# A decode kernel's ring of key and value slots: ten of 2 MB against five of 4 MB, with the output weights on a second queue

## The chip, the cores and the metric

The kernel runs on one core of one Trainium2 chip. Times are device microseconds of that core. A ratio is the mean time of one kernel's fast runs over that of the other's fast runs of the same rounds, so it is not quite the ratio of the medians that are quoted beside it. A 95% interval of a ratio is about 0.0015 either way here, or 4 us; single runs of one kernel mostly lie within 1 us of each other.

## The reference

One token (x, 512 numbers) goes through an attention block with 32 heads and a cache of 65,536 keys and values per head, and through a small gated feed-forward block; a gate mixes the two. Only the parts that matter:

```python
H, Sk, Dh = 32, 65536, 128                     # all arrays bf16
q = (x @ wq).reshape(1, 1, H, Dh)              # one query a head
scores = einsum("bhqd,bhkd->bhqk", q, k_cache) * Dh ** -0.5
o = einsum("bhqk,bhkd->bhqd", softmax(scores), v_cache)
a = o.reshape(1, 1, H * Dh) @ wo               # wo: 4096 x 512
b = (silu(x @ w_gate) * (x @ w_up)) @ w_down
out = g * a + (1 - g) * b                      # g = sigmoid((x * gate_w).sum())
```

K and V are 537 MB each and every byte is used once; all weights together are some 14 MB.

## The kernel before

It is written with hand-placed semaphores. SyncE issues all loads, in one fixed list, into a ring of ten slots of 2 MB (16 KB a partition). A row below is one contiguous run that a load moves into one partition; the trace has one record (a packet) for each row: 65,536 of 16 KB for the 512 loads of K and V, of 128 rows each. A slot holds 64 blocks of 128 keys. For a K slot, TensorE transposes 48 of the blocks and multiplies them with q, ScalarE copies the transposes out of PSUM, and VectorE scores the other 16 blocks by itself. V blocks follow some 15 groups behind. At the end come the projection with `wo`, one product a head, and the mix.

```python
NSLOT = 10; V_LAG = 2; ND = 16; SLOT = CB * 128           # CB = 64 blocks a slot
wo_dram = A_wo.rearrange("(h d) n -> d h n", d=Dh)        # rows of 512 numbers: 1 KB
def kv_src(t, i):                                         # 16 KB a partition, contiguous
    h, c = divmod(i, NCH)
    return t[0, h, c*CB*P:(c+1)*CB*P, :].rearrange("(p r) d -> p (r d)", p=P)

for s in range(NK - NCH - V_LAG, NK):                     # end of the job list
    if s == NK - NCH + min(2, NCH - 1):
        jobs += [("wo", i) for i in range(NOW)]           # NOW = 2
    jobs.append(("v", s))

# SyncE
for i, job in enumerate(jobs):
    if i >= NSLOT:
        for cond in free_of(jobs[i - NSLOT]):             # slot's last reader is done
            w(*cond)
    sp.dma_start(view(job), source(job)).then_inc(ld[i % NSLOT], 16)
# ... (cut)
# TensorE, end
while done_v < NV:
    if done_v == NV - VPC:                                # ahead of the last V slot
        w("s_otn", 1)
        for h in range(H - 1):
            out_proj(h)
    values(done_v)
    done_v += 1
```

## Time and profile before

| | before |
|---|---|
| time, median of 3 | 2,621.87 us (2,621.15 to 2,622.85) |
| bytes moved, mean rate over the span | 1,093 MB, 417 GB/s |
| TensorE, ScalarE, VectorE busy | 81%, 61%, 46% |
| last K or V byte, span of the trace | 2,609.0 us, 2,620.5 us |

First the page of the profile: the span, TensorE's busy time, the rate in 40 equal slices, packets, the share of each DMA queue (q1 is SyncE's queue, q8 fetches instructions), and the chain of work that ended last.

```profile
span 2620.5 us, 87632 instructions
...
PE 2120.4 (81%) x41281; PEld 2051.0 (78%) x41282; DVE 1208.0 (46%) x598; ACT 1585.7 (61%) x1607; POOL 25.3 (1%) x71
...
PE   6888878888888888888888888788787888888884
...
GB/s 397 425 424 425 425 426 425 425 425 425 426 424 426 424 426 425 425 426 425 425 422 422 421 421 419 421 420 424 419 419 420 418 424 419 421 420 418 421 370 276
DMA packets 81632, 1093.28 MB, mean 417 GB/s; under 512 B 8307, under 2 KB 14198, under 8 KB 15222
...
q1 hardware_dynamic: 81270, 1087.67, 98.6%
q8 instruction: 322, 5.28, 0.8%
...
DMA 82%; PE 15%; issue 1%; SPq 1%; ACT 1%; POOL 0%; DVE 0%; POOLq 0%; ACTq 0%
```

The loads bound it: the slices show a flat rate from beginning to end, and 82% of the chain is waiting for DMA. q8 deserves a look: 322 packets of 16 KB are 5.28 MB, and TensorE has 82,563 instructions (41,281 products and 41,282 weight loads), 256.4 for each packet.

Next the windows of the trace: busy time of each engine in a stretch, and at the end of the line the granted clock, the DMA share and GB/s.

```profile
400.00:1200.00 800.00, 658.25 (x12743) 642.54 (x12741) 372.60 (x179) 494.02 (x498) 6.25 (x20) 0.51 1.01 425
...
1600.00:2400.00 800.00, 656.58 (x12773) 641.19 (x12772) 374.35 (x180) 494.96 (x499) 6.41 (x20) 0.52 1.00 421
2541.00:2565.00 24.00, 15.35 (x400) 14.79 (x400) 5.57 (x4) 7.07 (x9) 0.64 (x2) 0.50 0.50 210
2577.00:2604.00 27.00, 7.47 (x256) 7.14 (x256) 0.00 (x0) 0.00 (x0) 0.00 (x0) 0.50 1.01 425
2609.00:2620.00 11.00, 8.95 (x91) 3.94 (x89) 0.90 (x2) 0.00 (x0) 0.00 (x0) 0.81 0.00 0
```

The rate is 425 GB/s early and 421 late. From 2,541 to 2,565 us it is 210, just half (the half-rate stretch). From 2,609 us on nothing is loaded.

What happens then is in the timeline of TensorE (start, duration, instruction):

```profile
2604.57 1.86 PE L442 MATMUL psT<-pcol,ring 128*128 128x1 bf16 x64 [2.89 <-DMA ring<-in_A_v_cache_dram]
2606.36 9.53 PE L470 MATMUL psT<-ring,oTn 128*1 128x512 bf16 x31
2615.82 1.75 PE L442 MATMUL psT<-pcol,ring 128*128 128x1 bf16 x64
2617.83 0.38 PE L496 MATMUL psT<-ring,oTn 128*1 128x512 bf16 x1 [0.26 <-DVE oTn L363]
```

The 31 projections (9.53 us) start only 2.6 us before the last V byte arrives, so the last V block waits behind them.

Last, the loads by line (KB each, median us from issue to landing). The last line is the output weights, on SyncE's queue like all others:

```profile
ring<-in_A_k_cache_dram SPq DMA_DIRECT2D x256, 2048.0 KB, 42.5
ring<-in_A_v_cache_dram SPq DMA_DIRECT2D x256, 2048.0 KB, 41.2
...
ring<-in_A_wo_dram SPq DMA_DIRECT2D x2, 2048.0 KB, 42.6
```

The single packet records of the trace, gathered by size, give the cost of a row of each length:

```
row         1,024 B   3,584 B   8,192 B   16,384 B   semaphore, 4 B   q8, 16,384 B
median ns        49       142       309        613                9          1,073
count         5,891     1,024       512     65,536            8,307            322
```

A 16 KB row begins 4 ns before the previous one ends, one in four takes 620 ns instead of 613, and the row that follows an instruction fetch takes 1,110 on average. No record names its DMA engine, but the rows in flight can be counted: sixteen in the stream (fifteen during a fetch), and in the half-rate stretch, where the DMA share is 0.50, eight, and seven during each of the three fetches that begin there (at 2,543.1, 2,551.2 and 2,557.6 us). So these fetches took the place of a row on one of the eight engines at work. The semaphore writes, 16 for each load, tell as much of the stream. From 200 to 1,200 us 125 fetches begin on q8; four trains of 204 writes each run through it with 4.89 to 4.91 us between writes, never set back, while others are set back 15 or 16 times (two followed 15 times, one 16), by 1.54 to 1.59 us, with one fetch begun each time. 125 fetches on eight engines are 15.6 each, on 16 they would be 7.8.

### The profile page before, as it was taken

What the parts mean: (1) busy time and instruction counts of PE and PEld (TensorE: products, weight loads), DVE (VectorE), ACT (ScalarE), POOL (GpSimd) and SP (SyncE); (2) the same over time, 40 slices, a digit from 0 to 9 for tenths busy, and PEclk for the clock granted to TensorE, in tenths of its full rate; (3) what the DMA queues carried; (4) which work ended last, traced back from release to release, by engine and by line L of the source; (5) the groups of instructions that cost most, each with busy time, mean ns of one, the idle gap of its engine ahead of it and who ended that gap; (6) DMA issues with size and microseconds to landing.
All of it is one profiled execution on the core that took longest, in us unless ns stands there. A gap on an engine that the chain in (4) does not pass through costs nothing.

```text
span 2620.5 us, 87632 instructions
## 1 busy us (share of the span) xinstructions
PE 2120.4 (81%) x41281; PEld 2051.0 (78%) x41282; DVE 1208.0 (46%) x598; ACT 1585.7 (61%) x1607; POOL 25.3 (1%) x71
## 2 busy tenths in 40 slices
PE   6888878888888888888888888788787888888884
PEld 4787777788778787878888878788787888787882
DVE  4744444444545454444444444444454444444440
ACT  4866666666666666666666666666666666666650
POOL 0000000000000000000000000000000000000000
PEclk8755565555555555555555555555555555555555
DMA  9999999999999999999999999999999999999986
GB/s 397 425 424 425 425 426 425 425 425 425 426 424 426 424 426 425 425 426 425 425 422 422 421 421 419 421 420 424 419 419 420 418 424 419 421 420 418 421 370 276
DMA packets 81632, 1093.28 MB, mean 417 GB/s; under 512 B 8307, under 2 KB 14198, under 8 KB 15222
## 3 DMA queue, kind: packets, MB, share of 16 engines
q1 hardware_dynamic: 81270, 1087.67, 98.6%
q8 instruction: 322, 5.28, 0.8%
q14 instruction: 40, 0.33, 0.0%
HBM read 1087.64 MB, written 0.00 MB: 415 GB/s over the span
## 4 chain that ended last, share of the span: by engine, by line
DMA 82%; PE 15%; issue 1%; SPq 1%; ACT 1%; POOL 0%; DVE 0%; POOLq 0%; ACTq 0%
DMA ring<-in_A_k_cache_dram 65%; DMA ring<-in_A_v_cache_dram 17%; PE psT L411 10%; PE psO L442 2%; PE psS L425 2%; SPq L220 1%; ACT KT L270 1%; PE psT L470 0%; PE psT L442 0%; PE psO L463 0%; PE psS L454 0%; POOL amx L235 0%; POOL nbias L237 0%; DVE finrow L366 0%; DVE mxs L338 0%
## 5 line engine op out<-in xcount | busy, mean ns | idle before, releaser
L270 ACT ACTIVATE KT<-psT 128x1024 bf16<-128x1024 bf16 x1536 | 1562.0, 1030 | 922.3 <-PE psT L411 921.7
L411 PE MATMUL psT<-ident,ring 128*128 128x128 bf16 x12288 | 1523.5, 303 | 412.1 <-DMA ring<-in_A_k_cache_dram 411.6
L411 PEld LDWEIGHTS psT<-ident,ring 128*128 128x128 bf16 x12288 | 1153.1, 137 | 432.8 <-DMA ring<-in_A_k_cache_dram 431.5
L329 DVE TENSOR_TENSOR prod<-ring,qbc 128x2048 f32<-128x2048 bf16 x256 | 586.7, 2292 | 1299.9 <-DMA ring<-in_A_k_cache_dram 1298.8
L442 PEld LDWEIGHTS psO<-pcol,ring 128*128 128x128 bf16 x15872 | 692.6, 111 | 54.0 <-DMA ring<-in_A_v_cache_dram 38.0
L442 PE MATMUL psO<-pcol,ring 128*128 128x1 bf16 x15872 | 690.2, 169 | 26.9 <-DMA ring<-in_A_v_cache_dram 25.4
L331 DVE TENSOR_REDUCE sD<-prod 128x16 f32<-128x2048 f32 x256 | 585.2, 2286 | 8.7
L425 PE MATMUL psS<-qTb,KT 128*128 128x1 bf16 x12288 | 540.9, 165 | 10.1 <-ACT KT L270 5.8
L425 PEld LDWEIGHTS psS<-qTb,KT 128*128 128x128 bf16 x12288 | 445.8, 104 | 18.2 <-ACT KT L270 17.7
L442 PE MATMUL psT<-pcol,ring 128*128 128x1 bf16 x512 | 14.8, 165 | 34.2 <-DMA ring<-in_A_v_cache_dram 34.2
L442 PEld LDWEIGHTS psT<-pcol,ring 128*128 128x128 bf16 x512 | 14.2, 103 | 35.2 <-DMA ring<-in_A_v_cache_dram 31.6
L251 ACT ACTIVATE pcol<-psS,nbias 128x512 bf16<-128x512 f32 x32 | 21.9, 684 | 30.2 <-POOL nbias L237 30.2
L235 POOL PARTITION_ALL_REDUCE amx<-mxs x32 | 14.1, 440 | 2236.9 <-DVE mxs L338 2236.9
L363 DVE TENSOR_TENSOR oTn<-psT,Li 128x1 bf16<-128x1 f32 x1 | 0.2, 161 | 49.8 <-PE psT L442 49.8
L338 DVE TENSOR_REDUCE mxs<-psS 128x1 f32<-128x512 f32 x32 | 22.1, 691 | 1.1
L258 ACT ACTIVATE qbc<-psT 128x512 bf16<-128x512 f32 x4 | 2.4, 597 | 21.2 <-PE psT L392 21.2
L237 POOL TENSOR_SCALAR nbias<-amx 128x1 f32<-128x1 f32 x32 | 10.0, 313 | 289.8 <-issue 289.8
L384 PE MATMUL psS<-xTb,ring 128*128 128x1 bf16 x128 | 3.6, 165 | 11.4 <-DMA ring<-in_A_wq_dram 11.4
L336 DVE COPY psS<-sD 128x128 f32<-128x128 f32 x32 | 9.1, 284 | 7.9 <-PE psS L425 7.9
L384 PEld LDWEIGHTS psS<-xTb,ring 128*128 128x128 bf16 x128 | 3.5, 104 | 11.5 <-issue 11.5
L470 PE MATMUL psT<-ring,oTn 128*1 128x512 bf16 x31 | 9.5, 481 | 0.0
L392 PE MATMUL psT<-ring,xb 128*128 128x512 bf16 x31 | 8.4, 438 | 0.2 <-issue 0.2
(39 smaller groups left out, 35.0 us busy)
## 6 DMA issues: line engine op xcount, KB each, us to landing
ring<-in_A_k_cache_dram SPq DMA_DIRECT2D x256, 2048.0 KB, 42.5
ring<-in_A_v_cache_dram SPq DMA_DIRECT2D x256, 2048.0 KB, 41.2
ring<-in_A_wq_dram SPq DMA_DIRECT2D x2, 2048.0 KB, 10.0
ring<-in_A_wo_dram SPq DMA_DIRECT2D x2, 2048.0 KB, 42.6
ring<-in_B_w_gate_dram SPq DMA_DIRECT2D x1, 1792.0 KB, 21.8
ring<-in_B_w_up_dram SPq DMA_DIRECT2D x1, 1792.0 KB, 25.7
ring<-in_B_w_down_dram SPq DMA_DIRECT2D x1, 1792.0 KB, 30.2
xrow<-in_A_x_dram SPq DMA_DIRECT2D x1, 1.0 KB
```

Source lines behind the costliest of these rows:

```text
L220: sp.dma_start(view(job), source(job)).then_inc(ld[i % NSLOT], 16)
L235: nc.gpsimd.partition_all_reduce(amx[:, h:h + 1], mxs[:, h:h + 1], P, RMAX).then_inc(sm["s_ar"], 1)
L237: nc.gpsimd.tensor_scalar_mul(nbias[:, h:h + 1], amx[:, h:h + 1], -SCALE).then_inc(sm["s_nb"], 1)
L251: nc.scalar.activation(pcol[:, h % 2, :], psS[:, h % 2, 0:NC_H], ACT.Exp, bias=nbias[:, h:h + 1], scale=SCALE, accum_out=rsum[:, h:h + 1]) ...
L270: nc.scalar.activation(KT[:, g % NKT, :], kt_ps(g), ACT.Copy, bias=0.0).then_inc(sm["ev_a"], 1)
L329: nc.vector.tensor_tensor(prod[:], kb, qb, ALU.mult).then_inc(sm["s_tt"], 1)
L331: nc.vector.reduce_sum(sD[:, h % 2, j * ND:(j + 1) * ND], prod[:], AX_X).then_inc(sm["s_rd"], 1)
L338: nc.vector.reduce_max(mxs[:, h:h + 1], psS[:, h % 2, 0:NC_H], AX_X).then_inc(sm["s_mx"], 1)
L411: last = nc.tensor.transpose(dst[:, k * 128:(k + 1) * 128], src[:, b * 128:(b + 1) * 128], ident[:])
L425: last = mm(psS[:, h % 2, col:col + 1], KT[:, g % NKT, k * 128:(k + 1) * 128], qTb[:, h:h + 1], start=True, stop=True)
L442: last = mm(acc, src[:, b * 128:(b + 1) * 128], pcol[:, h % 2, col:col + 1], start=(j == 0 and b == 0), stop=(j == NCH - 1 and b == CB - 1))
L470: mm(psT[0:1, 0, 0:D], oTn[:, h:h + 1], view(("wo", h // HO))[:, h % HO, :], start=(h == 0), stop=(h == H - 1))
```

## The change

Its intent is fewer and longer rows: five slots of 4 MB with 32 KB a partition. Along with it `wo` moves to ScalarE's queue, the projection moves ahead of the penultimate V slot, the last V slot comes in 3.5 + 0.5 MB, x and gate_w come transposed through ScalarE's queue, and the other weights are laid out in long rows. The core of the diff:

```diff
-NSLOT = 10
+CB_MAX = 128
+NSLOT = 5
+SHARE = 4
+DB = 16
-V_LAG = 2
+V_LAG = 1
+TAIL = 16
-    CB = min(64, NC_H)
+    CB = min(CB_MAX, NC_H)
+    ND = CB // SHARE                  # 32 of 128 blocks on VectorE, as two of 16
-        wd_dram = B_w_down.rearrange("(c p) n -> p c n", p=P)
+        wd_dram = B_w_down.rearrange("(p c) n -> p c n", p=P)   # also wq, w_gate, w_up
-        for s in range(NK - NCH - V_LAG, NK):
-            if s == NK - NCH + min(2, NCH - 1):
-                jobs += [("wo", i) for i in range(NOW)]
-            jobs.append(("v", s))
+        rest = [("v", s) for s in range(NK - NCH - V_LAG, NK)]
+        early = max(0, len(rest) - (NSLOT - NOW))
+        jobs += rest[:early] + [("wo", i) for i in range(NOW)] + rest[early:]
+            if job == ("v", NK - 1):
+                cut = (CB - TAIL) * 128
+                return [(dst[:, 0:cut], src[:, 0:cut]), (dst[:, cut:], src[:, cut:])]
 # SyncE
-            sp.dma_start(xrow[0:1, :], ...); sp.dma_start(gwrow[0:1, :], ...)
+            for job in jobs:
+                if job[0] != "wo":
+                    load(sp, w, job)
 # ScalarE
+            act.dma_start(xT[:, 0:Dc], ...); act.dma_start(gwT[:, 0:Dc], ...)
 ... (cut: softmax, copies out of PSUM)
+            for job in jobs:
+                if job[0] == "wo":
+                    load(act, w, job)
             softmax(H - 1)
 # TensorE
-                if done_v == NV - VPC:
-                    w("s_otn", 1)
-                    for h in range(H - 1):
-                        out_proj(h)
+                if done_v in proj_at:          # ahead of the penultimate slot
+                    out_proj(proj_at[done_v])
 ... (cut: slot views, gate by two small products, VectorE in halves)
```

## The prediction

> **What bounds it.** The loads. The chain of waits is 82% DMA; the page moves 1,093 MB at 417 GB/s, DMA share 1.0 in nearly every slice; TensorE is 81% busy, ScalarE 61%, VectorE 46%, and they wait for K (VectorE 1,299 us). A faster engine gives nothing.
>
> The packet records give more. A 16 KB row takes 613 ns and the next starts 4 ns before its end; an 8 KB row takes 309: almost no cost per packet is left. Every fourth descriptor is 7 ns longer, and the 4-byte semaphore write costs about 6 ns a transfer. By my reading the instruction fetches (322 of 16 KB, second queue) fall on half of the 16 DMA engines: each takes 1,066 ns and the load packet after it 1,110, about 1.5 us of its engine, some 60 us for each of eight. That half sets the pace. The other runs ahead: the windows show 425 GB/s to 1,200 us, then 421 when the lead has used up the ring, and 210 (eight engines) from 2,541 to 2,565 us, when the next V slots wait for the last head's softmax. Estimate for a lagging engine: 4,096 packets x 611.7 ns + 62 us of fetches + 35 us of weights = 2,603 us, near where the stream ends (2,608). So the half-rate stretch costs little.
>
> After the last byte 11.5 us remain: 31 projections begun at 2,606.4 take 9.5 us, then the last V block, the row and the store.
>
> **What the change does.**
> 1. 32 KB rows, half the descriptors: saves (estimate) 22 ns, perhaps 30 more, of 9,868 per 4 MB: 6 us, at most 15, all critical. If rows are split into 16 KB packets, nothing.
> 2. w_down in 14 KB instead of 1 KB rows: 1 us.
> 3. Projection ahead of the penultimate V slot and a 0.5 MB tail: after the last byte only 16 products, one projection (0.4), the row (0.7) and the store: 4 us instead of 11.5. Saves 7.
> 4. First transfer issued 0.7 us earlier.
> 5. Five slots of 4 MB hold the same bytes. K is held about 22 us, V 16 us, of 39 us before the slot is needed (estimate from TensorE's load): no slot comes late.
> 6. The last V loads no longer wait for the last softmax: as argued, worth little.
> 7. The risk: the output weights (4 MB in 1 KB rows, 256 packets an engine) come through ScalarE's queue beside V's 32 KB rows. [...] Here a load packet after another queue's packet takes 376 to 490 ns more. If turns are by single rows, the weights end after the last V: 33 turns x 0.4 us, plus the projection and two V slots behind it, some 35 us lost. If a turn takes many small rows, nothing. The same holds for x and gate_w in 8-byte pieces at the start (0 to 6 us). I hold the benign case likelier, 2 to 1.
>
> **Prediction.** Benign 2,601 us, bad 2,637. I say 2,603 us, range 2,588 to 2,635; over 2% faster 0.03, within 2% 0.94, over 2% slower 0.03.
>
> **What would show it.** K and V packets of 32 KB at about 1,220 ns; 422 to 424 GB/s late in the run; no half-rate stretch; the end 4 us after the last V byte; output weights landing before V's penultimate slot. Wrong if: 32 KB packets take under 1,215 ns (faster), the weights' landing takes over 50 us, ScalarE's last exponential waits behind its own issue, or fetches cost less between larger packets.

That two queues take turns, and how many rows a turn has, was the author's assumption: in the kernel before, all loads are on one queue, and no run had shown it. Nor had one shown whether a 32 KB row would stay one packet. The 376 to 490 ns are measured there: a 16 KB row takes 378 ns more (median) after an 8 KB fetch of q14, another instruction queue, and 489 more after one of q8.

## The result, and the profile after

| | before | after |
|---|---|---|
| time, median | 2,621.93 us | 2,612.85 us (2,612.24 to 2,613.41) |
| ratio | | 0.9965 (0.9948 to 0.9982) |
| span of the trace | 2,620.5 us | 2,610.4 us |
| last K or V byte | 2,609.0 us | 2,580.3 us |
| last byte of any load | 2,609.0 us | 2,590.3 us |
| from there to the end | 11.6 us | 20.0 us |

The time lies within the range, but the gain is 9 us where 19 were predicted. The page after:

```profile
span 2610.4 us, 87113 instructions
...
PE 2090.8 (80%) x41279; PEld 2035.5 (78%) x41280; DVE 1204.8 (46%) x597; ACT 1580.7 (61%) x1607; POOL 101.2 (4%) x71
...
GB/s 410 426 426 429 428 427 427 428 427 426 428 423 426 421 424 424 424 422 423 422 423 425 423 423 422 423 424 423 422 423 423 421 426 419 425 421 425 425 387 258
DMA packets 42344, 1093.23 MB, mean 419 GB/s; under 512 B 4481, under 2 KB 8578, under 8 KB 8706
...
q1 hardware_dynamic: 37586, 1083.46, 97.8%
q8 instruction: 322, 5.28, 0.8%
q10 hardware_dynamic: 4400, 4.20, 0.5%
...
DMA 68%; PE 28%; issue 1%; DVE 1%; another core or an unknown queue 1%; ACT 0%; POOL 0%; ACTq 0%; POOLq 0%
```

The rate is up a little in most slices (in ten of the 40 it is lower, by 1 to 4 GB/s and in the last by 18) and there are half as many packets (a row of 32 KB stayed one: the trace has 32,768 of them). A new queue, q10, stands for ScalarE's loads. The chain is less DMA (68%) and more TensorE (28%). It does not say that TensorE got slower, as its busy time fell by 30 us; that much of it is a matter of names, since TensorE now waits for V where it waited for K, is a reading that no run tested.

The windows:

```profile
400.00:800.00 400.00, 328.11 (x6413) 322.89 (x6411) 187.12 (x90) 248.36 (x251) 15.80 (x10) 0.50 1.00 427
1600.00:2400.00 800.00, 652.28 (x12831) 641.33 (x12829) 374.30 (x180) 495.82 (x502) 34.59 (x21) 0.51 1.00 423
2544.00:2574.00 30.00, 9.67 (x339) 9.36 (x339) 0.55 (x2) 0.78 (x2) 0.81 (x2) 0.50 1.00 415
2574.00:2591.00 17.00, 0.05 (x1) 0.09 (x2) 0.00 (x0) 0.00 (x0) 0.00 (x0) 0.50 0.83 283
2591.00:2611.00 20.00, 16.77 (x288) 9.77 (x287) 0.90 (x2) 0.00 (x0) 0.00 (x0) 0.67 0.01 2
```

423 GB/s late instead of 421. At the end a tail appears: from 2,574 to 2,591 us the loads run at 283 GB/s, and TensorE does nothing (0.05 us). Then it is busy 16.8 us of the last 20.

The chain of waits at the end (start, duration, what it was):

```profile
2566.02 24.79 another core or an unknown queue
...
2590.95 9.50 PE psT L509 x31
2600.45 6.75 PE psT L479 x256
...
2607.43 0.60 PE psT L533
```

"Another core or an unknown queue" is here the transfer on ScalarE's queue, the output weights. TensorE waits 24.79 us for them. Only then come the 31 projections, both V slots behind them (256 products), and the last projection. TensorE's timeline says it by name:

```profile
2590.95 9.50 PE L509 MATMUL psT<-ring,oTn 128*1 128x512 bf16 x31 [24.93 <-DMA ring<-in_A_wo_dram]
2600.38 6.80 PE L479 MATMUL psT<-pcol,ring 128*128 128x1 bf16 x256
2607.43 0.59 PE L533 MATMUL psT<-ring,oTn 128*1 128x512 bf16 x1 [0.25 <-DVE oTn L400]
```

Lines answering to those of the loads before (the third is the large part of the last V slot):

```profile
ring<-in_A_k_cache_dram SPq DMA_DIRECT2D x128, 4096.0 KB, 34.7
...
ring<-in_A_wo_dram ACTq DMA_DIRECT2D x1, 4096.0 KB, 50.2
ring<-in_A_v_cache_dram SPq DMA_DIRECT2D x1, 3584.0 KB, 32.2
```

A 4 MB load on SyncE's queue lands in some 30 us. The output weights, issued at 2,540.6 us, take 50.2.

The packet records show why. Of the 1 KB rows of the weights, 376 were read from 2,544 to 2,571 us, beside 337 of V's rows of 28 or 32 KB: nearly one for one. When the large part of the last V slot had landed at 2,578.6 us, 2,877 of the 4,096 rows of the weights were still to come; they took to 2,590.3. At the start it is the same: x comes in 128 rows of 8 bytes, as does gate_w, and from 4 to 22 us 221 of ScalarE's small rows were read beside 220 rows of 32 KB of the other queue. x landed 13.6 us after its issue and gate_w 23.9; in the kernel before both were there at 2.5 us.

So here the two queues took turns row by row (376 beside 337, 221 beside 220), which was the case that the prediction held to be the less likely. But V's rows of 32 KB that began from 2,544 to 2,571 us took only 1,253 ns on average (1,237 in the stream from 1,000 to 2,000 us, fetches included), not the 0.4 us more that the prediction had taken from rows after an instruction fetch.

### The profile page after: what moved, and what is told of

It reads as the page before. It is cut to its first block, busy times and chain, and to the rows that moved or that the text cites. A ratio compares the mean times of both kernels' runs of the same rounds, so it can differ in the third digit from the quotient of the medians.

```text
span 2610.4 us, 87113 instructions
## 1 busy us (share of the span) xinstructions
PE 2090.8 (80%) x41279; PEld 2035.5 (78%) x41280; DVE 1204.8 (46%) x597; ACT 1580.7 (61%) x1607; POOL 101.2 (4%) x71
## 4 chain that ended last, share of the span: by engine, by line
DMA 68%; PE 28%; issue 1%; DVE 1%; another core or an unknown queue 1%; ACT 0%; POOL 0%; ACTq 0%; POOLq 0%
DMA ring<-in_A_v_cache_dram 67%; PE psT L444 17%; PE psO L479 5%; PE psS L460 4%; DMA gwT<-in_gate_w_dram 1%; DVE prod L371 0%; DVE sD L374 0%; PE psT L479 0%; ACT KT L304 0%; PE psT L509 0%; PE psT L425 0%; PE psS L494 0%; PE psS L418 0%; PE psO L502 0%
## 5 line engine op out<-in xcount | busy, mean ns | idle before, releaser
L479 PEld LDWEIGHTS psO<-pcol,ring 128*128 128x128 bf16 x15872 | 703.1, 112 | 450.1 <-DMA ring<-in_A_v_cache_dram 349.6
L267 POOL PARTITION_ALL_REDUCE amx<-mxs x32 | 71.8, 2242 | 2085.2 <-DVE mxs L381 2085.2
L269 POOL TENSOR_SCALAR nbias<-amx 128x1 f32<-128x1 f32 x32 | 28.3, 883 | 357.2 <-issue 357.2
L479 PEld LDWEIGHTS psT<-pcol,ring 128*128 128x128 bf16 x512 | 13.8, 102 | 12.5 <-ACT pcol L285 9.4
## 6 DMA issues: line engine op xcount, KB each, us to landing
ring<-in_A_k_cache_dram SPq DMA_DIRECT2D x128, 4096.0 KB, 34.7
ring<-in_A_v_cache_dram SPq DMA_DIRECT2D x127, 4096.0 KB, 29.4
ring<-in_A_wo_dram ACTq DMA_DIRECT2D x1, 4096.0 KB, 50.2
```

The source lines that it names most:

```text
L267: nc.gpsimd.partition_all_reduce(amx[:, h:h + 1], mxs[:, h:h + 1], P, RMAX).then_inc(sm["s_ar"], 1)
L269: nc.gpsimd.tensor_scalar_mul(nbias[:, h:h + 1], amx[:, h:h + 1], -SCALE).then_inc(sm["s_nb"], 1)
L479: last = mm(acc, src[:, b * 128:(b + 1) * 128], pcol[:, h % 2, col:col + 1], start=(j == 0 and b == 0), stop=(j == NCH - 1 and b == CB - 1))
```

## The experiments

Twelve kernels were run, all timed over five rounds against the kernel before. Theory A: the row-by-row turns put the weights behind V, and TensorE's order makes two V slots wait for them. Theory C: TensorE's instruction fetches fall on eight of the 16 DMA engines, and those set the pace of the stream. Their rivals are named with each run.

| run | median us | ratio to before (95%) | last byte of a load | end after it |
|---|---|---|---|---|
| changed kernel | 2,612.85 | 0.9965 (0.9948 to 0.9982) | 2,590.3 | 20.0 |
| e1_wo_sp | 2,599.75 | 0.9916 (0.9903 to 0.9930) | 2,592.1 | 6.0 |
| e2_proj_last | 2,606.72 | 0.9943 (0.9929 to 0.9957) | 2,592.7 | 12.5 |
| e3_rows16_sp | 2,621.16 | 0.9999 (0.9987 to 1.0012) | 2,613.8 | 6.0 |
| e4_one_tail | 2,601.19 | 0.9922 (0.9908 to 0.9935) | 2,591.5 | 7.2 |
| e5_pe_more | 2,636.94 | 1.0056 (1.0039 to 1.0074) | 2,631.1 | 7.0 |
| e6_pv_thin | 2,577.85 | 0.9832 (0.9819 to 0.9844) | 2,572.1 | 3.9 |
| e7_share48 | 2,596.78 | 0.9902 (0.9890 to 0.9915) | 2,589.8 | 5.9 |
| e8_share64 | 2,618.30 | 0.9987 (0.9974 to 0.9999) | 2,606.9 | 6.0 |
| f1_x_sp | 2,613.37 | 0.9967 (0.9952 to 0.9981) | 2,592.0 | 20.3 |
| f2_share48_x_sp | 2,593.74 | 0.9894 (0.9881 to 0.9906) | 2,586.0 | 5.9 |
| f3_best | 2,593.37 | 0.9889 (0.9876 to 0.9901) | 2,586.7 | 4.8 |
| g1_pe_more48 | 2,601.78 | 0.9922 (0.9908 to 0.9936) | 2,594.4 | 6.0 |

The last two columns are from the profiled run of each.

### e1_wo_sp: the output weights back on SyncE's queue

```diff
 # SyncE
             for job in jobs:
-                if job[0] != "wo":
-                    load(sp, w, job)
+                load(sp, w, job)
 # ScalarE
-            for job in jobs:
-                if job[0] == "wo":
-                    load(act, w, job)
             softmax(H - 1)
```

> The changed kernel with one part undone: the output weights are issued by SyncE again, in their place of the job list. Theory A (row-by-row turns between two queues let the weights land 8 us after the last V byte, and TensorE, which projects ahead of the penultimate V slot, then has 9.5 us of projection and 6.8 us of V products behind them): the weights land before V, nothing but 16 products and one projection follows the last byte, and the time is 2,592 to 2,597 us. Rival B (the DMA engines that carry the instruction fetches are busy to the end anyway, so the place of the weights does not matter): 2,609 to 2,614 us, as the changed kernel.

It took 2,599.75 us, 13.1 less than the changed kernel. TensorE's timeline at the end:

```profile
2575.03 9.23 PE L505 MATMUL psT<-ring,oTn 128*1 128x512 bf16 x31
2584.19 3.41 PE L475 MATMUL psT<-pcol,ring 128*128 128x1 bf16 x128
2591.32 3.57 PE L475 MATMUL psT<-pcol,ring 128*128 128x1 bf16 x128 [3.72 <-DMA ring<-in_A_v_cache_dram]
2595.15 0.58 PE L529 MATMUL psT<-ring,oTn 128*1 128x512 bf16 x1 [0.25 <-DVE oTn L396]
```

The projections now start at 2,575.0, 16 us earlier, while V still comes in, and end before the last slot is there. That is what theory A said, and it is shown: this one edit is worth 13 us. The time missed the expected stretch by 3 us, in two places. The end is 6.0 us after the last byte and not 4 (see e4). And the last byte came no sooner than in the changed kernel (2,592.1 against 2,590.3 us), so the turns cost the DMA engines next to nothing: rival B was right on that half. What was lost was TensorE's work, put behind a transfer that came last.

Two windows of the same run show the half-rate stretch again, and the end:

```profile
2539.00:2545.00 6.00, 5.61 (x162) 5.52 (x159) 0.99 (x2) 3.04 (x3) 0.38 (x1) 0.50 0.52 171
2592.00:2598.00 6.00, 3.48 (x110) 2.89 (x107) 0.90 (x2) 0.00 (x0) 0.00 (x0) 0.50 0.01 3
```

From 2,539 to 2,545 us only 1 KB rows were read, about 165 in a microsecond, at a DMA share of 0.52. A row takes 46 to 48 ns, so (estimate) 165 x 0.047 = 7.8, some eight engines, were at it, and eight had nothing to do.

### e2_proj_last: the projection after all V products

```diff
             while done_v < NV:
-                if done_v in proj_at:
-                    out_proj(proj_at[done_v])
                 values(done_v)
                 done_v += 1
+            for i in range(NOW):
+                out_proj(i)
```

> The changed kernel (weights still from ScalarE) with the 31 projections after all V products instead of ahead of the penultimate slot. Theory A: the weights still land near 2,591 us, V's products are done by then, and only 9.5 us of projection and about 3 us of ending follow: 2,604 to 2,607 us, so projecting ahead costs some 7 us as long as the weights come late. If the order of TensorE's work does not matter: 2,612 to 2,614 us.

2,606.72 us, 6.1 less than the changed kernel, as theory A has it: the V products are done before the weights land, and the projections alone wait for them.

```profile
2581.59 3.57 PE L479 MATMUL psT<-pcol,ring 128*128 128x1 bf16 x128 [6.94 <-DMA ring<-in_A_v_cache_dram]
2593.33 9.39 PE L509 MATMUL psT<-ring,oTn 128*1 128x512 bf16 x31 [8.16 <-DMA ring<-in_A_wo_dram]
```

Projecting early is right when the weights are early (e1) and wrong when they are late: the changed kernel combined the early projection with the queue that makes the weights late.

### e3_rows16_sp: five slots of 4 MB, but rows of 16 KB

Each slot's load is cut into its two halves, on e1_wo_sp (the waits count 32 instead of 16):

```diff
-            return [(dst, src)]
+            half = CB * 64
+            return [(dst[:, 0:half], src[:, 0:half]), (dst[:, half:], src[:, half:])]
```

> As e1_wo_sp, but every 4 MB K or V slot comes in two transfers of 16 KB a partition row. Theory A (the gain in the stream is from half as many descriptors: 1,216 against 2 x 613 ns, one 7 ns stretch in every four descriptors, one semaphore write a transfer, together 70 ns per 4 MB or 18 us): 14 to 18 us slower than e1_wo_sp. Rival B (the gain is from the five larger slots or from the other weights' layout): within 3 us of e1_wo_sp.

2,621.16 us: 21.4 more than e1_wo_sp, a little over the expected 14 to 18, and as slow as the kernel before. The window of the late stream:

```profile
1600.00:2400.00 800.00, 641.69 (x12730) 631.59 (x12727) 370.37 (x179) 491.00 (x498) 30.68 (x20) 0.53 1.00 419
```

419 GB/s, where the changed kernel has 423. So the longer rows, in transfers twice as large, carry all of the stream's gain (the run halves both and does not separate them), and larger slots with the old rows are no better than the ten small ones, rather worse: the last byte comes at 2,613.8 us against 2,609.0. The records account for 18 us (estimate): rows overlap by 4 ns, so a 32 KB row costs 1,212 ns and two of 16 KB 1,218, which is 48 ns per 4 MB; the 7 ns stretches and the semaphore writes, half as many, make some 22 more; 70 ns times 256 slots. The rest of the 21.4 us is open; rows of 16 KB that met no fetch took 614.5 ns on average instead of 614.2, which is 1.4 us of it.

### e4_one_tail: the last V slot in one transfer

```diff
-            if job == ("v", NK - 1):
+            if False:                      # and no wait for the tail's semaphore
```

> As e1_wo_sp, but the last V slot comes in one transfer. If the ending counts, 128 products (3.6 us) instead of 16 (0.5 us) follow the last byte: 2.5 to 3.5 us slower than e1_wo_sp. If TensorE is late anyway: the same as e1_wo_sp.

2,601.19 us: 1.4 more than e1_wo_sp, half of what was expected. The timeline of e1_wo_sp above has the reason: at 2,591.32 TensorE makes all 128 products of the last slot in one go (3.57 us). Its wait ended with the large first part, which landed only 1.3 us before the 0.5 MB tail (2,590.84 and 2,592.11 us in the packet records), so 112 products, not 16, were left at the end. So the tail was worth about the time that it takes to load, here 1.3 us.

### e6_pv_thin: fewer TensorE instructions

On e1_wo_sp:

```diff
-                for k in range(GB):
+                for k in (0, GB - 1):      # two V products of eight
```

> As e1_wo_sp, wrong on purpose: of every eight V products only the first and the last are made, 24,576 fewer TensorE instructions and all loads as before. Theory C: 96 fewer fetches, 18 us faster than e1_wo_sp (9 us if spread over 16 engines), about 2 us of it the shorter last V block on top. Rival D, bytes: only those 2 us.

2,577.85 us, 21.9 less than e1_wo_sp, with the very same loads. (The comparison with the reference doesn't notice the thinned sum, and the kernel is not valid.) q8 and the late window:

```profile
q8 instruction: 226, 3.70, 0.6%
```

```profile
1600.00:2400.00 800.00, 473.54 (x9112) 459.07 (x9112) 374.51 (x181) 479.77 (x507) 29.32 (x20) 0.71 1.00 426
```

322 fetches became 226, and 423 GB/s became 426. The last byte came 20.0 us earlier (the rest is the shorter last V block): 0.21 us for each of the 96 fetches. Theory C expected 1.53 us / 8 = 0.19; spread over 16 engines it would have been 0.10. The rows of V and K themselves took 1,216 ns as before, so TensorE's fewer products made no row faster. Rival D falls. One rival was not named: with fewer products the slots also come free sooner. It is not likely: the K and V loads of e1_wo_sp landed 34.7 and 29.4 us after their issue (medians), and one slot takes 9.9 us at 423 GB/s, so as a rule (estimate) two loads were already queued in front, and a slot that is free sooner would not have helped the DMA engines that are behind.

### e5_pe_more and g1_pe_more48: more TensorE instructions

```diff
+                for _ in range(12):
+                    pe.wait_ge(sm["s_ident"], 1)     # satisfied long ago
                 for k in range(GB):                  # one group of transposes
```

> As e1_wo_sp, with 12 waits that are already satisfied ahead of every group of transposes: 9,216 more TensorE instructions and not a byte or a product more. Theory C (TensorE's instruction fetches, 16 KB for each 256 instructions, cost 1.04 us on their DMA engine and 0.49 us more for the load packet after them, and all fall on the same eight engines, which set the pace): 36 more fetches x 1.53 / 8 = 6.9 us slower than e1_wo_sp, or 3.4 us if they are spread over all 16. Rival D (the pace is set by bytes, or by the compute engines' use of the on-chip memory): within 1 us of e1_wo_sp.

2,636.94 us, 37 more, and with runs from 2,627 to 2,647. The 36 more fetches came (358 on q8), but TensorE itself was now late. Two lines of its waits:

```profile
PE psT L442 <- issue: 152.7, 282, 2.2
...
PE psO L477 <- issue: 104.1, 105, 2.7
```

Where e1_wo_sp waits 415 us in total for V, this run hardly waits for data and stands 328 us in "issue". It is inconclusive for theory C. It was repeated on f2_share48_x_sp (below), where TensorE has more room:

> f2_share48_x_sp with the 12 satisfied waits of e5_pe_more ahead of each of its 1,280 groups of transposes, some 7,700 more TensorE instructions: e5_pe_more repeated where TensorE has room (72% busy instead of 80%), since there TensorE itself became late. Theory C (instruction fetches on eight engines set the pace): 30 more fetches x 1.53 us / 8 = 5.7 us slower than f2_share48_x_sp, 2,598 to 2,601 us (2.9 us if all 16 engines share them). Rival D (bytes set the pace): 2,593 to 2,595 us. If it is 10 us or more slower, TensorE is late again and the run says nothing of the fetches.

2,601.78 us, 8.0 more than f2_share48_x_sp, with 30 more fetches (320 against 290):

```profile
q8 instruction: 320, 5.24, 0.8%
```

TensorE still waited 311 us for K and 128 us for V, so it was not late on the whole. The direction is theory C's; the time is just over the expected 2,598 to 2,601 us, and the size, 0.27 us a fetch, is above its 0.19. Some 75 us of new "issue" waits may hold the rest, which is not shown. Together with e6: fewer fetches, faster; more fetches, slower; no byte of data changed in either.

### e7_share48 and e8_share64: fewer TensorE instructions, right result

On e1_wo_sp, VectorE scores more blocks of each K slot:

```diff
-    ND = CB // SHARE
+    ND = 3 * CB // 8        # e7: 48 blocks     (e8: CB // 2, 64 blocks)
```

> As e1_wo_sp, right result: VectorE scores 48 of the 128 blocks of a K slot instead of 32, so TensorE makes 16 fewer transposes and 16 fewer score products a slot, 8,192 fewer instructions. Theory C: 32 fewer fetches, 6 us faster than e1_wo_sp, 2,593 to 2,595 us. Rival D: the same as e1_wo_sp. VectorE rises from 46% to about 69% busy and is not in the way.

> As e7_share48 with 64 of 128 blocks on VectorE: 16,384 fewer TensorE instructions than e1_wo_sp. Theory C: 64 fewer fetches, 12 us faster than e1_wo_sp, 2,587 to 2,589 us, if VectorE keeps up (estimate 18.6 us of work in each 19.8 us). If VectorE frees the K slots too late, slower than e7_share48.

e7 took 2,596.78 us, 3.0 less than e1_wo_sp where 6 were expected. Its window from 120 to 200 us:

```profile
120.00:200.00 80.00, 72.81 (x1464) 72.57 (x1465) 71.84 (x34) 54.76 (x57) 2.56 (x2) 0.50 0.94 397
```

397 GB/s there instead of 428: VectorE, busy 90% of this stretch, started at 38 us, after gate_w had come, and gave its first slots back late. e8 took 2,618.30 us: the same loss at the start is larger (332 GB/s from 120 to 200 us), and its last byte came 14.7 us later than e1's (VectorE is 94% busy from 2,500 to 2,540 us, and the loads fall to 340 GB/s in the 40 us after). The expectation "12 us faster" failed: VectorE kept up in the middle (426 GB/s from 400 to 2,400 us) but not at the two ends.

### f1_x_sp, f2_share48_x_sp and f3_best: x and gate_w first on SyncE's queue

```diff
 # ScalarE
-            act.dma_start(xT[:, 0:Dc], ...); act.dma_start(gwT[:, 0:Dc], ...)
 # SyncE, first
+            sp.dma_start(xT[:, 0:Dc], ...);  sp.dma_start(gwT[:, 0:Dc], ...)
```

> The changed kernel with x and gate_w (128 rows of 8 bytes each) issued by SyncE ahead of the first weights instead of by ScalarE beside them; the output weights still come from ScalarE. x then lands at about 3 us instead of 13.5, gate_w at 3 instead of 25. If the late start costs time, or the turns between the two queues slow the first loads: 3 to 6 us faster than the changed kernel. If the ring hides the late start (the page shows 428 GB/s from 20 to 200 us): within 1 us, 2,612 to 2,614 us.

On the changed kernel this gives 2,613.37 us, no difference. The late x and gate_w cost the changed kernel nothing: the first contents of its five slots had come at 46.7 us, and the next K load was issued into the first free slot by 38.4 us, so the loads didn't have to wait.

> e7_share48 with x and gate_w issued by SyncE ahead of the first weights. e7_share48 gained 3 us over e1_wo_sp where 6 were expected of 32 fewer instruction fetches, and its windows show 421 and 397 GB/s from 60 to 200 us, an estimated 7 us of loading lost. If that loss comes from VectorE's late start (its first product at 38 us, after gate_w), it goes away here: 2,589 to 2,592 us. If it has another cause: 2,596 us as e7_share48.

On e7_share48 it gives 2,593.74 us, 3.0 less by the medians, where 5 to 8 were expected (the four runs of each overlap: 2,593.4 to 2,595.4 and 2,594.2 to 2,597.6). The loss at the start shrank but is still there:

```profile
120.00:200.00 80.00, 68.73 (x1486) 67.63 (x1484) 73.14 (x34) 53.34 (x55) 2.56 (x2) 0.59 0.98 413
```

413 instead of 397 GB/s. So the late start was part of e7's shortfall. That the rest is VectorE's larger share, which is behind at first in any case, was not tested.

> f2_share48_x_sp with the last transfer of V twice as large (32 blocks). In e1_wo_sp TensorE starts the 112 blocks of the first part only when the last part is about to land, and makes 128 products in a row (3.6 us). With 96 blocks in the first part it starts about 1.3 us earlier: 1 to 1.5 us faster than f2_share48_x_sp. If the two parts land together whatever their sizes: the same.

f3 has `TAIL = 32`. 2,593.37 us is within the noise of f2: no gain. In f3's trace TensorE came late from the projections (they ended at 2,580.9) and the last 128 products began at 2,584.75, again in one go.

f3_best is right, and faster than both kernels: 0.9889 of the kernel before (0.9876 to 0.9901), 28.5 us by the medians. f2, without the larger tail, does as well.

## Why the prediction was wrong

The range held the time (2,612.85 in 2,588 to 2,635) but the predicted gain, 19 us, was twice the measured one.

- **The step that failed is item 7**, "I hold the benign case likelier, 2 to 1". The bad case happened: the turns were by single rows (376 weight rows beside 337 V rows), and the weights landed 10 us after the last V byte. e1_wo_sp puts its cost at 13.1 us. The prediction had itself named "the weights' landing takes over 50 us" as a sign against it: it took 50.2.
- **The benign case was well aimed.** It was 2,601 us; e1_wo_sp, which makes the weights come in time, measured 2,599.75. That the sum is right is in part luck: rows and ending missed in opposite directions, as below.
- **The bad case was mis-sized**: "some 35 us lost" against 13.1. The term "33 turns x 0.4 us" (13 us) measured about nothing: V's rows took 1,253 ns in that stretch against 1,237 in the stream. The 376 to 490 ns that a row took longer after an instruction fetch did not carry over to two queues of loads here. What remained is TensorE's 9.5 us of projection and 6.8 us of V products behind the weights, less what the end costs in any case.
- **Item 1, the rows**: "6 us, at most 15, all critical". e3_rows16_sp against e1_wo_sp says 21.4 us. Of this, 4.8 us only make up for what the larger slots lose with the old rows: from the kernel before to e1_wo_sp the last byte came 16.9 us earlier. The packet length was right (about 1,220 foreseen, 1,216 measured); the term was too small because what a long row saves by itself, 6 ns of 1,218 (two 16 KB rows against one of 32 KB, each counted from the end of the one before less the 4 ns of overlap) or 48 ns per 4 MB, was taken as a mere chance of "perhaps 30 more".
- **Item 3, the ending**: "4 us instead of 11.5" became 20.0 us in the changed kernel, by item 7, and 6.0 in e1_wo_sp. The two extra are the 112 products that the tail could not hide (e4: the tail is worth 1.4 us).
- **The reading of what bounds it held up.** Instruction fetches on half of the engines were foreseen as the pace: e6_pv_thin and g1_pe_more48 changed the number of fetches and no byte of the other loads, and the time moved by 0.21 and 0.27 us a fetch; eight engines would give 0.19, all 16 0.10. That the fetches fall on the eight engines that lag is shown in the kernel before by the count of rows in flight (eight in the half-rate stretch, seven during each of its three fetches; eight too in the changed kernel, from 2,537.2 to 2,542.0 us) and from 200 to 1,200 us by the trains of semaphore writes (four never set back, three set back 15 or 16 times). For the other fetches it is taken from these. The records also show the lead running out. In the kernel before, rows that follow no fetch are longer than usual by 1 to 2 us in all in each 200 us from 200 to 1,200 us, and by 30 to 40 us from 1,400 us on. The 25 fetches of such a stretch cost 25 x 1.56 = 39 us (estimate from 1,067 ns and the 497 ns of the row after it), so from then on the other eight engines lose about as much as the eight with the fetches.
- **"The half-rate stretch costs little"** and **item 6** were not tested, since every run has the stretch. They fit the above: the eight engines at work in it are those that lag, and the last byte of the loads came at 2,590.3 to 2,592.7 us in the changed kernel, e1, e2, e4 and f1 alike.
- **"422 to 424 GB/s late in the run"** held (423). **"No half-rate stretch"** did not: the changed kernel still runs at 262 GB/s from 2,535 to 2,544 us.

In this trace a turn was one row, 1 KB on one side and 28 or 32 KB on the other (376 beside 337). The queue of the output weights changed the last byte of all loads little (2,590.3 against 2,592.1 us), but not who got bytes first: the weights took 50.2 us from issue to landing on ScalarE's queue and 30.0 on SyncE's, and here that was 13 us. And 2 MB transfers with 16 KB rows cost 21 us in 2,600 against 4 MB with 32 KB rows (e3_rows16_sp), whichever of the two it is.

## What to carry to other kernels

Here a second queue did not share bandwidth by bytes: it got about one row for each row of the other (376 beside 337), so a load in short rows beside a stream in long rows landed when the stream was over. Keep such a load in the stream's own queue, ahead of what it is needed for (13 us here), or put the work that needs it behind the work whose data come first (6 us here). When a kernel is bound by loads, count the instructions of its busiest engine as well: here they were loads too (322 fetches of 16 KB; each of the 96 that e6_pv_thin saved was worth 0.21 us of the whole time).
